# A state-space scan with a Gelu MLP on one core: weight quarters loaded and used in turns, decay rows in four blocks, first B load moved forward

## The chip, the cores and the metric

The kernel runs on one core of one Trainium2 chip. The metric is device time in microseconds (us), taken as the median of several runs. The engines are TensorE (PE in the profile; its weight loads are PEld), VectorE (DVE), ScalarE (ACT), GpSimd (POOL) and SyncE (SP), which here only issues DMAs. Each engine works through its own queue strictly in the order in which the program lists it.

## The reference, cut to what matters

There are 4 batches of 8 heads, 768 positions, 32 values per head and 16 state values. The first half is a scan with decay, the second a two-layer MLP over its output; `B`, `C`, `x` and `a` are inputs.

```python
for c in range(nc):
    cum = np.cumsum(la, axis=-1)
    L = np.exp(cum[:, :, :, None] - cum[:, :, None, :]) * causal
    M = np.einsum('bhin,bhjn->bhij', Cc, Bc) * L
    y = np.einsum('bhij,bhjd->bhid', M, xc) + np.einsum('bhin,bhnd->bhid', Cc, state) * np.exp(cum)[..., None]
    Bx = np.einsum('bhjn,bhjd->bhjnd', Bc, xc) * decay_from_j[:, :, :, None, None]
    state = decay_full[:, :, None, None] * state + np.sum(Bx, axis=2)
h = x @ w_in
g = 0.5 * h * (1.0 + np.tanh(c * (h + 0.044715 * h * h * h)))
return (g @ w_out).astype(np.float32)
```

In the second half `x` is the scan's output as 3072 tokens of 256 values; `w_in` is 256 x 2048 and `w_out` 2048 x 256. All inputs are float32; the kernel multiplies in bfloat16 and sums in float32.

## The kernel before, in words

**Tiles.** Positions are cut into chunks of 128, 6 for each batch, 24 in all. Two chunks (256 tokens) form a unit, so there are 12 units, 3 for each batch. A step is called by its function and its indices: `Y.1` is the second scan product of unit 1, `s1.2.3` the first matmul of the MLP in unit 2, piece 3.

**The scan.** Rows of `a` are clipped and run backwards through a product scan on DVE (`clipq` and `Rq` for chunks 0 to 3 of all batches, from `load_aq`; `clip` and `R` for the long rows, from `load_a`, line 340 for both scans). The results are turned by 32x32 transposes on DVE (`tpq`, `tp2`, `tp6`, line 351), and reciprocals are taken (`recip0`, `recip1`, `recip`). `B` is multiplied by the decay and `C` by its reciprocal (`mulb`, `mulc`, `mul1`, `mul`; for batch 0, chunks 0 to 3 in `BC0[0]`, chunks 4 and 5 in `BC0[1]`). PE transposes the products (`tw`, `T1`, `T`), and copies take them out of PSUM (`ew`, `ce1`, `bh1`, `E`, `F`). For batch 1, `N` turns `B` back and `bn` copies it; batches 2 and 3 are transposed through DRAM by DMA (`load_wr`, `load_tr`, `load_bn`). `G` makes the products of C and B for a unit, four banks of PSUM in two tiles (`ga`, `gb`), `M` multiplies two banks by the triangular mask (line 613, DVE). In unit 0 the second tile goes by ACT (`GE`, a copy) and POOL (`ME`, a select) instead. `D` or `XD` makes the new state terms, `S` adds them up (line 684), `SP` spreads a state over the heads (line 691), and `Y` sums both parts into the PSUM bank `yb`. `yev` copies the result to `xm`, in bfloat16.

**The MLP.** `s1.u.i` is four matmuls (line 717) into one of two buffers `hp` in PSUM, `gelu.u.i` (ACT, line 721) takes them to `gT`. `s2.(u).(k).(q)` is four matmuls of unit u, chunk k, with quarter q of `w_out` (line 735), into a bank `o_ps` (near the end also into `yb`). It needs `gelu.u.2q` and `gelu.u.(2q+1)`. `oev` copies a chunk's sum out of PSUM and `store` writes it. There are 96 steps `s1` and 96 steps `s2`; here they are called pieces. Weights come in quarters of 512 KB (`load_wi`, `load_wo`), each cast to bfloat16 by two steps (`wi.q.k`, `wo.q.k`). `s1.u.0` and `s1.u.1` need quarter 0 of `w_in`, the next two quarter 1, and so on.

**Order.** The steps are issued in an order that is written out by hand in the string `ORDERED`. A letter behind a colon sets the engine (A for ACT, D for DVE, P for POOL, S for SP), otherwise the engine is the one in `add(...)`. `~59` stands for 59 blocks of 128 columns of idle matmuls (`fill`, line 705). `wl`, `bl`, `xl` are load steps on SP's queue, which issues loads, stores and DMA transposes in one row. A DMA's start therefore waits for all that stands ahead of it on SP. From unit 3 to unit 10, `D` and `G` of the next unit are issued inside `Y`.

**What the steps of the change touch.** The order of unit 0 to unit 2 on PE, up to `G.3`, the first product of batch 1, is this:

```
~59 tw.1 tw.2 ~4 tw.0 ~2 G.0 ~1 ppq XX.0 XD.0 ~17 Y.0 XX.1 XD.1 s1.0.0 G.1 s1.0.1 ... s1.0.6 Y.1 pp
s1.0.7 s1.1.0 T1.0 s1.1.1 T1.1 N1 s1.1.2 s1.1.3+10 G.2 s1.1.4 s1.1.5 s2.0.0.0 D.2 s2.0.1.0 s1.1.6
T.1.1 s1.1.7 Y.2 T.1.0 s1.2.0 s1.2.1 N.1 s1.2.2 G.3 D.3
```

`XX` and `XD` for units 0 and 1 leave the transposed `x` and the state terms in PSUM (`XN`), in the bank `o_ps` and in buffers of `hp`. `c_warm` is one Gelu on one column, the first activation of the program; `c_unp` and `c_sel` make constants on DVE.

## Time and profile before

| what | value |
|---|---|
| median of 3 runs | 118.75 us |
| lowest and highest run | 118.48 and 119.01 us |
| span of the profiled execution, first to last instruction | 116.9 us |
| between that span and the median | 1.85 us |
| PE busy | 110.1 us, 1426 matmuls |
| DVE, ACT, POOL busy | 69.4, 72.1, 21.4 us |
| DMA | 15.97 MB, 43007 packets, 36657 of them under 512 B |

The span is the profiled execution's own time as the page gives it; the median also holds what lies around the span. The granted clock of TensorE is 1.000 throughout. The page cuts the span into 40 slices of 2.92 us and gives the busy share of each engine in tenths. The chain is the row of work that ended last, followed back from the last instruction. A time at the left of a line is counted from the span's start.

### The profile page before, as it was taken

How to read it: one execution, taken by the hardware profiler on the slowest of the kernel's cores; microseconds unless marked ns; L12 is line 12 of the kernel's file. 1: busy time of each engine (PE TensorE's matmuls, PEld its weight loads, DVE VectorE, ACT ScalarE, POOL GpSimd, SP SyncE). 2: the span in 40 equal slices, each digit the busy share in tenths (PEclk: the TensorE clock that was granted, in tenths of full speed). 3: DMA queues.
4: the chain of work that ended last, by engine and by line, in shares of the span. 5: the costliest groups of instructions: out<-in, count | busy, mean ns of one | idle time of the engine just before them, and what ended most of it. 6: DMA issues, size and time to landing. Idle time of an engine off the chain costs nothing.

```text
span 116.9 us, 3379 instructions
## 1 busy us (share of the span) xinstructions
PE 110.1 (94%) x1426; PEld 92.0 (79%) x1426; DVE 69.4 (59%) x140; ACT 72.1 (62%) x139; POOL 21.4 (18%) x38
## 2 busy tenths in 40 slices
PE   6988999998899999999999999999999999999990
PEld 2354676776789979989898999889798998999970
DVE  5898899899785936716695583049493462101020
ACT  2249899968486459565766677828465587447501
POOL 7606816908206000052200000000000000000000
PEclk9999999999999999999999999999999999999999
DMA  0999997999983929998407472044201201101113
GB/s 26 228 332 357 281 252 178 208 288 257 305 143 90 185 47 219 213 253 200 72 25 171 121 163 63 0 140 98 40 6 63 71 0 52 43 0 50 45 47 132
DMA packets 43007, 15.97 MB, mean 137 GB/s; under 512 B 36657, under 2 KB 41457, under 8 KB 42993
## 3 DMA queue, kind: packets, MB, share of 16 engines
q1 hardware_dynamic: 42800, 15.64, 56.0%
q8 instruction: 11, 0.18, 0.6%
q10 hardware_dynamic: 192, 0.13, 0.5%
q14 instruction: 4, 0.02, 0.1%
HBM read 11.04 MB, written 3.93 MB: 128 GB/s over the span
## 4 chain that ended last, share of the span: by engine, by line
PE 75%; DMA 8%; DVE 6%; SPq 6%; issue 2%; POOL 1%; ACT 0%; DVEq 0%; POOLq 0%
PE o_ps L735 33%; PE hp L717 30%; DMA bcf<-in_B_dram 8%; PE yb L735 3%; SPq L190 3%; PE ga L603 3%; PE yb L658 2%; DVE m L613 2%; PE yb L667 2%; DVE ce L523 1%; SPq L150 1%; DVE bh L327 1%; DVE bc L484 1%; SPq L159 1%; SPq L183 1%
## 5 line engine op out<-in xcount | busy, mean ns | idle before, releaser
L721 ACT ACTIVATE gT<-hp 128x512 bf16<-128x512 f32 x96 | 54.3, 596 | 25.0 <-PE hp L717 24.6
L717 PE MATMUL hp<-xm,w_in_sb 128*128 128x256 bf16 x384 | 53.3, 273 | 0.6 <-ACT gT L721 0.4
L735 PE MATMUL o_ps<-w_out_sb,gT 128*128 128x256 bf16 x352 | 47.3, 273 | 0.0
L717 PEld LDWEIGHTS <-w_in_sb 128*128 128x128 bf16 x384 | 41.4, 114 | 3.5 <-issue 1.9
L735 PEld LDWEIGHTS <-gT 128*128 128x128 bf16 x384 | 37.0, 98 | 4.9 <-issue 1.1
L327 DVE COPY o_sb<-o_ps 128x256 f32<-128x256 f32 x13 | 5.5, 425 | 23.8 <-PE o_ps L735 20.4
L613 DVE TENSOR_TENSOR m<-ga,tri 128x1024 bf16<-128x1024 f32 x12 | 14.6, 1218 | 0.1
L613 DVE TENSOR_TENSOR m<-gb,tri 128x1024 bf16<-128x1024 f32 x11 | 13.4, 1219 | 0.7 <-PE gb L603 0.7
L323 ACT ACTIVATE o_sb<-o_ps 128x256 f32<-128x256 f32 x9 | 3.5, 385 | 9.2 <-PE o_ps L735 9.2
L705 PE MATMUL yb<-wz 128*128 128x512 bf16 (+3 forms) x23 | 7.6, 481 | 1.1 <-DVE wz L220 1.1
L691 DVE SCALAR_TENSOR_TENSOR sp_new<-s_new,pend,bmask 128x256 bf16<-128x256 f32 x17 | 7.9, 476 | 0.0
L327 DVE CAST xm<-yb 128x512 bf16<-128x512 f32 x6 | 4.1, 687 | 5.8 <-PE hp L636 4.8
L684 DVE SCALAR_TENSOR_TENSOR s_new<-s_new,pend,hp 128x64 f32<-128x64 f32 x13 | 3.6, 279 | 6.4 <-PE hp L636 6.2
L705 PEld LDWEIGHTS <-wz 128*128 128x128 bf16 x26 | 3.0, 120 | 5.1 <-issue 3.2
L667 PE MATMUL yb<-m,x 128*32 128x128 bf16 x192 | 6.1, 220 | 0.0
L603 PE MATMUL ga<-ce,bh 32*128 32x256 bf16 x48 | 4.7, 273 | 1.3 <-DVE bn L327 0.9
L484 POOL TENSOR_TENSOR bc<-bc_t,pt 128x768 bf16<-128x768 f32 x2 | 3.0, 1494 | 13.8 <-DMA bc_t<-in_C_dram 13.7
L658 PE MATMUL yb<-ce,sp_new 128*32 128x128 bf16 x160 | 5.3, 221 | 0.0
L603 PE MATMUL gb<-ce,bh 32*128 32x256 bf16 x48 | 4.7, 273 | 0.0
L735 PE MATMUL yb<-w_out_sb,gT 128*128 128x256 bf16 x32 | 4.6, 273 | 0.0
L667 PEld LDWEIGHTS <-x 128*32 128x32 bf16 x192 | 3.8, 97 | 0.8 <-issue 0.8
L323 ACT ACTIVATE xm<-yb 128x512 bf16<-128x512 f32 x6 | 3.6, 595 | 1.1 <-PE hp L636 1.1
(115 smaller groups left out, 79.5 us busy)
## 6 DMA issues: line engine op xcount, KB each, us to landing
out_dram<-o_sb SPq DMA_DIRECT2D x24, 128.0 KB, 1.9
x_t<-in_x_dram SPq DMA_DIRECT2D x20, 128.0 KB, 3.9
wf<-in_moe_w_in_dram SPq DMA_DIRECT2D x4, 512.0 KB, 6.7
wf<-in_moe_w_out_dram SPq DMA_DIRECT2D x4, 512.0 KB, 5.5
bc_t<-in_C_dram SPq DMA_DIRECT2D x3, 384.0 KB, 5.8
bc_t<-in_B_dram SPq DMA_DIRECT2D x3, 384.0 KB, 5.5
scr<-bc SPq DMA_DIRECT2D x4, 192.0 KB, 2.2
x_t<-in_x_dram SPq DMA_DIRECT2D x1, 512.0 KB, 5.8
```

The source lines that it names most:

```text
L323: nc.scalar.activation(o, i, AF.Copy)
L327: nc.vector.tensor_copy(out=o, in_=i)
L484: (nc.gpsimd if eng == "POOL" else nc.vector).tensor_tensor(out=d["bc16"][:, i], in0=d["bc"].rearrange("p i h (r n) -> p i r h n", r=R6)[: ...
L603: nc.tensor.matmul(out=gbank(g)[:, 256 * k:256 * k + 256], lhsT=bh_of(2 * u + k)[gs], rhs=ce_of(2 * u + k)[gs], start=True, stop=True, til ...
L613: nc.vector.tensor_tensor(out=m_of(u)[:, 2 * i:2 * i + 2].rearrange("p g k e t -> p (g k e) t"), in0=gx[i].rearrange("p g (k t) -> p (g k) ...
L658: nc.tensor.matmul(out=y4[32 * j:32 * j + 32, k, w], lhsT=sp[:, 32 * h:32 * h + 32], rhs=ce_of(gc)[:, h % 2], start=first(j), stop=False, ...
L667: nc.tensor.matmul(out=y4[32 * j:32 * j + 32, k, w], lhsT=X16[u][:, k, 32 * h:32 * h + 32], rhs=m[:, h // 2, h % 2, :], start=first(j), st ...
L691: nc.vector.scalar_tensor_tensor(out=sp_new.rearrange("p (g d) -> p g d", g=4), in0=(XN[0][:, H * D:H * D + 64] if gc == 0 else state[("s" ...
L705: nc.tensor.matmul(out=t[:, 0:m * 128], lhsT=wz, rhs=w3.to_broadcast([128, m, 128]), start=True, stop=True, skip_group_check=True)
L717: nc.tensor.matmul(out=hp[:, j * T:(j + 1) * T], lhsT=w_in_k[:, w, q, k], rhs=xm[:, w, u * T:(u + 1) * T], start=(w == 0), stop=(w == 1))
L721: nc.scalar.activation(gts[u][:, 2 * i:2 * i + 2], hps.pop((u, i)).rearrange("p (j t) -> p j t", j=2), AF.Gelu_apprx_tanh)
L735: nc.tensor.matmul(out=ops[gc], lhsT=gts[u][:, fi, k * Q:(k + 1) * Q], rhs=w_out_sb[:, fi, :], start=(fi == 0 and (u > 0 or k == 0)), stop ...
```

## The change

**Loads.** On SP's queue the load of B for the first four chunks (`load_bc0.0`) is issued first, ahead of two of the four loads of the first decay rows (`load_aq.1`, `load_aq.3`; the other two are on ACT's queue). The quarters of `w_in` and `w_out` then take turns with other loads: `wi.0 wi.1 wo.0 bc1(C) wi.2 bc1(B) wi.3 wo.1 x.2(half) wo.2 x.2(half) bc.1(C) bc.1(B) x.3(half) wo.3`. Before, it was `wi.0 wi.1 wi.2 wi.3 bc1(C) bc1(B) wo.0 x.2 bc.1(C) bc.1(B) x.3 wo.1 wo.2 x.4 wo.3`. A unit's `x` becomes two steps.

**Long decay rows.** `a_t` held 64 rows of 384; now it holds four blocks of 32 rows in 128 partitions, 192 positions each, with the last two chunks behind them in columns 256 to 383. Four DMAs load it, all on ACT's queue. `tp2` is one transpose where it was four, `tp6` one of 128x192 where it was four of 32x192, and the reciprocals of batches 1 to 3 are three steps.

**Uses.** In units 0 and 1 `s2` goes by quarters: both chunks of a unit share a bank (unit 0 `o_ps`, unit 1 `yb`) and take quarter 0, then quarter 1, and so on. `XX.1` goes to the banks of `gb`. `M` of unit 0 on `gb` is one bank on DVE (`MD.0.3`) and one by ACT and POOL; for unit 1 both banks of `gb` go by ACT and POOL. `Y.0` is issued in halves. `mulb` is cut in two, `x4` in four.

**Engines.** Among others, `c_unp` and the second half of `c_sel` go to ACT, the mask `bmask` to DVE; `wi.0.0`, `wi.2.1`, `wi.3.1`, `wo.1.0`, `castx.2`, `ce1`, `bh1`, `bn1`, `mul.1.1` and `E.1.1` are on DVE. `c_warm` stands between `Y.10` and `gelu.9.1`, so the first activation is a Copy. The order of all later units is new as well.

The order on PE up to `G.3` is now this (`Yw` is half of `Y.0`):

```
~47 tw.0 tw.1 tw.2 ~6 G.0 ppq ~12 XX.0 XD.0 G.1 Yw.0.0 Yw.0.1 s1.0.0 s1.0.1 XX.1 XD.1 s1.0.2 s1.0.3
s2.0.0.0 s2.0.1.0 s1.0.4 s1.0.5 T1.1 Y.1 T1.0 pp s1.0.6 s1.0.7 G.2 s2.0.0.1 s1.1.0 s1.1.1 s2.0.1.1
s1.1.2 N1 s2.0.0.2 s2.0.1.2 D.2 s1.1.3 s1.1.4 Y.2 s1.1.5 s1.1.6 T.1.1 s2.1.0.0 s1.1.7 s1.2.0 s2.1.1.0
s2.1.0.1 T.1.0 s1.2.1 s2.1.1.1 s2.1.0.2 s2.1.1.2 N.1 s1.2.2 s2.0.0.3 D.3 G.3
```

The diff, cut to its core:

```diff
+c_wz load_aq.2 load_aq.0 c_ident c_tri c_sel c_sub c_m4 load_bc0.0 load_a.0 c_zero load_aq.1
+load_aq.3 c_az c_ends load_bc0.1 load_x4 c_unz clipq Rq tpq recip0 load_a.2 c_cz mulb.0 load_a.1
+c_unp ~47 mulb.1:P mulc.0 mulc.1:P load_a.3 c_selp tw.0 tw.1 load_wi.0 tw.2 x4.0:P ew.0.0:A ew.0.2
+peq load_wi.1 x4.1:P ew.1.0 ew.0.1 ew.1.1:A ~6 G.0 c_bmask:D load_wo.0 load_bc1.1 ew.1.2 load_wi.2
+load_bc1.0 ppq x4.2 x4.3 pendq MD.0.3 c_m16 GE.0.2 ~12 XX.0 xn.1 M.0.0 xn.0 XD.0 SP.0 S.0.0
+load_wi.3 G.1 ME.0.2 Yw.0.0 GE.1.3 wi.0.0:D Yw.0.1 yev.0.1.2 wi.0.1 load_wo.1 load_x.2.0 GE.1.2
...
+s1.0.2 gelu.0.1 ME.1.2 load_wo.2 load_x.2.1 xn.3 S.1.0 tp2 s1.0.3 c_par s2.0.0.0.o wi.2.1:D S.1.1
+wi.2.0 recip1 s2.0.1.0.o pe SP.1 SP.2 mul1.1:P gelu.0.2 xn.2 gelu.0.3 s1.0.4 load_bc.1.1 s1.0.5
+mul1.0:P T1.1 ce1.1:D wi.3.0 wi.3.1:D Y.1 gelu.0.4 wo.1.1 T1.0 pp ce1.0:D load_bc.1.0 gelu.0.5 pend
+bh1:D load_x.3.0 s1.0.6 yev.1.0.2 wo.2.0 wo.1.0:D s1.0.7 load_wo.3 G.2 tp6 gelu.0.6 gelu.0.7
...
-    a_t = const.tile([64, HS], FP32, name="a_t")
+    a_t = const.tile([128, AL], FP32, name="a_t")
...
     def f_tp2():
-        for k in range(4):
-            turn(rt0[1][32 * k:32 * k + 32], r_t[32:64, Q + 64 * k:Q + 64 * k + 64], 2)
+        turn(rt0[1], r_t[:, 2 * Q:2 * Q + Q // 2], 2)
...
+    def f_tp6():
+        turn(rt, r_t[:, 0:QL], R6)
...
+            XN[c] = gx[1][:, k] if u else pso.tile([128, 512], FP32, name="o_ps") if k == 0 else psh.tile([128, 512], FP32, name="hp")
...
+    def f_MD(u, g):
+        nc.vector.tensor_tensor(out=m_of(u)[:, g].rearrange("p k e t -> p (k e) t"),
+                                in0=gbank(g).rearrange("p (k t) -> p k t", t=Q), in1=tri_b(4), op=ALU.mult)
...
+            if u < 2:
                 if k == 0:
-                    ops["0"] = pso.tile([128, 512], FP32, name="o_ps")
+                    ops["u"] = yb if u else pso.tile([128, 512], FP32, name="o_ps")
...
-        for k, q in [(k, q) for q in range(4) for k in range(2)] if u == 0 else [(k, q) for k in range(2) for q in range(4)]:
+        for k, q in [(k, q) for q in range(4) for k in range(2)] if u < 2 else [(k, q) for k in range(2) for q in range(4)]:
```

## The prediction

> **What bounds the kernel now.** I read the page's busy slices first, then a table of busy time by stage, then the chain, then the DMA landings.

> ```profile
> PE   6988999998899999999999999999999999999990
> DVE  5898899899785936716695583049493462101020
> DMA  0999997999983929998407472044201201101113
> ```

> Each digit is 2.92 us in tenths. PE is full from the eleventh slice on; the first ten hold its only gaps, and there DVE and DMA are full.

> ```profile
> 10.00:12.46 2.46, 2.46 (x101) 1.33 (x93) 1.97 (x5) 2.37 (x6) 1.97 (x3) 1.00 1.04 394
> 12.46:18.90 6.44, 5.99 (x78) 4.52 (x78) 5.88 (x14) 5.86 (x13) 2.52 (x5) 1.00 0.96 213
> 18.90:24.00 5.10, 4.84 (x49) 3.50 (x49) 4.50 (x8) 4.67 (x11) 4.29 (x6) 1.00 1.15 212
> 24.00:29.69 5.69, 4.51 (x73) 3.67 (x72) 5.60 (x9) 4.09 (x7) 2.79 (x5) 1.00 1.03 293
> 29.69:113.90 84.21, 84.18 (x1080) 75.25 (x1079) 43.43 (x76) 50.61 (x94) 5.01 (x5) 1.00 0.44 100
> ```

> Columns: length, then PE, PEld, DVE, ACT, POOL busy. From 29.69 PE is busy 84.18 of 84.21 us, so **the end is the start of G.3 plus what PE still has to do then**. Just before, DVE is busy 5.60 of 5.69. The chain shows what G.3 waits for:

> ```profile
> 27.74 1.44 DVE ce L523 x2
> 29.17 0.48 DVE bn L327
> 29.69 0.28 PE ga L603 x2
> ...
> 37.91 1.75 PE o_ps L735 x16
> ```

> DVE's `F.1` and `bn.1` release G.3. The last line prices a piece: 16 matmuls in 1.75 us, four in 0.4375.

> **Pieces ahead of G.3.** By the two orders on PE, 19 steps `s1` and 2 `s2` stood ahead of G.3; now 19 and 13, and `D.3` (0.17, chain row at 30.09). PE's last matmul ends at 113.88, 84.19 after G.3. Of that, 11 x 0.4375 + 0.17 = 4.98 moves ahead. If G.3 started when it does now, the gain would be 4.98. All depends on how much later it starts. I follow the new queues with durations of these rows.

> **The first loads.** Landings, read as issue plus time to landing: `bc0` 5.2 and 6.4, `x4` 8.6, the quarters of `w_in` 9.9, 11.5, 12.9, 14.3, `bc1` 14.7 and 16.65, `wo.0` 18.2, `bc.1` 21.75 (C) and 23.3 (B), `wo.1` 26.2, `wo.2` 27.6. The stream is gapless, so a load costs the step between landings: 1.2 for a half of bc0, 2.2 for x4, 1.4 for a quarter, 1.15 for a half of bc1, 0.75 for half of an x, 1.7 for a half of bc.1. B goes out at 0.81, 0.92 before the first bc0 load now (1.73, landing 3.5 later), so it lands at 4.3 and the stream runs about 0.8 earlier. The two aq loads behind it lie between 3.5 (issue 1.73 plus their 1.8 unhindered) and 4.5 (behind all of B); I take 4.4. DVE now reaches `clipq` at 4.25 straight from `unp`, which goes to ACT; so clipq starts 0.15 later, while `mulb` and `mulc`, halved between DVE (0.42) and POOL (0.62), win 0.35. ACT takes `unp` (four at about 0.2) and `selp` while it waits for `tw` until 6.99 anyway. G.0 comes at 7.9 (now 8.13). x4 lands at 7.9 instead of 8.6, and halves of `x4`, `M.0` and `Y.0` run side by side: s1.0.0 at about 11.85 (now 12.46). The four `load_a` cost ACT's queue two more issues (0.32 to 0.44 each) before 6.9, where it idles; the `x` halves cost SP nothing new, each unit had two DMAs.

> **The weights in turns.** By the same steps: wi.0 9.3, wi.1 10.7, wo.0 12.2, wi.2 14.8 (1.9 later than now), wi.3 17.3 (3.0 later), wo.1 18.9 (7.3 earlier), wo.2 21.1, bc.1 23.5 (C, 1.75 later) and 25.1 (B), wo.3 27.3. So unit 0 waits for wi.3 and its casts: s1.0.6 at 18.1. Until then PE runs six s1 pieces and two s2. Then stand 24 pieces and 2.2 of G.2, Y.2, D, T and N before G.3: 12.7 us, which makes 30.8 the earliest G.3.

> **DVE up to G.3.** Removed:

> ```profile
> 16.93 1.94 DVE L351 STREAM_TRANSPOSE rt<-r_t 32x192 f32<-32x192 f32 x6
> 19.29 1.07 DVE L351 STREAM_TRANSPOSE rt<-r_t 32x192 f32<-32x192 f32 x2
> ```

> These eight become a 128x64 (0.24, as 32x64) and a 128x192 (0.54, as 32x192): -2.2; a cost by partitions is excluded by 128x128 at 0.41. Reciprocals 1.03 become two of 0.44 before F.1: -0.15. `M.1` on gb leaves: -1.2. `xn.0`, `yev.2`: -1.1. Added: MD 0.63, bmask about 0.7 (a reduce like 0.37 and a copy), `yev` half 0.42, casts wi.0.0, wi.3.1, wo.1.0, castx.2 1.7 (wi.2.1 replaces wi.3.0), ce1 0.82, bh1 and bn1 0.8, mul.1.1 0.95 (was POOL), E.1.1 0.96 (was ACT): +7.0. Net +2.3, less the 0.6 idle that DVE has at 22: 1.7 by the sum. Followed in order: SP.2 ends 17.2, M.2 22.2, SP.4 24.1, mul.1.1 starts 24.55 (after C landed at 23.5), E.1.1 27.0, mul.1.0 27.95, E.1.0 29.5, F.1 30.95, bn.1 31.45; G.3 at 31.65, with PE ready at 31.45. Both arrive together: **1.96 later than now**. ACT and POOL have idle stretches on this way and set nothing.

> **Two prices that the trace doesn't hold.** First, DVE casts beside POOL casts:

> ```profile
> 1.92 1.19 DVE L282 COPY selp<-sel 128x128 f32<-128x128 f32 x1
> 15.75 0.42 DVE L327 CAST w_in_sb<-wf 128x512 bf16<-128x512 f32 x1
> 27.65 1.52 DVE L523 TENSOR_SCALAR ce<-ch,par 128x768 bf16<-128x768 bf16 x2
> ```

> The cast at 15.75 ran with POOL idle. The selp copy ran beside a POOL memset, and this F pair beside POOL casts, where one of its form takes 0.41 at best: a stretch of 0.35 each. Of five DVE casts, wi.2.1, wi.3.1 and wo.1.0 are released by the same load as a POOL cast: 3 x 0.35 = 1.05; but F.1 now comes when POOL has finished its casts: -0.70. I take +0.4; bounds -0.7 and 5 x 0.77 = 3.85 (selp's 1.19 against 0.42). [...]

> Second, the first activation is now a Copy. Before, one table load (1.28, at 2.21) stood ahead of the Gelu of `c_warm`. If the load for Copy doesn't serve Gelu, a second one of 1.28 stands before gelu.0.0. The row of pieces up to s1.0.6 has 0.85 of slack, which leaves 0.4. Bounds 0 and 1.28; I take 0.4. [...]

> **After G.3.** The units' order is new, but PE's work is the same and ACT and DVE are half idle (43.43 and 50.61 of 84.21). The tightest place I find is Y.5: 12 pieces (5.25) after Y.4, against 4.9 of DVE work (S, two M, two SP, F.2). I add nothing. The fills dropped (about 2 us) stood in gaps. The tail is the same.

> **Sum.** G.3 at 31.65 + 0.4 + 0.4 = 32.45, 2.76 later; 2.76 - 4.98 = -2.2. The span of 116.9 becomes 114.7; with the 1.85 that lie between span and median, 118.75 becomes **116.5**.

> **Rivals.**
> - *PE's bound.* If casts don't collide, one table load suffices and loads are 0.5 earlier, G.3 comes at 30.3 to 31, 1.0 later than now: 114.7. For it: 30.8 above; against: DVE needs 31.65 by itself.
> - *Late loads.* bc.1 has 1 MB more ahead of it. If C lands 2.8 later than I think (26.3; SP's issues stall up to 3.4 us in this stretch), mul.1.1 waits 1.75 more, G.3 comes at 34.2 and gives back most of the gain: 118.3. Against it: the stream's own steps.
> - [...] At DVE, 11 to 31 us, all five casts pay 0.77: G.3 at 31.65 + 0.4 + 3.85 = 35.9, 6.2 later, 1.2 slower: 120.0. It decides from 0.52 for each cast (4.98 - 1.96 - 0.4 = 2.6). For it: the selp row; against: the F pair.
> - *No effect.* If the moved s2 pieces only wait for wo.1 and wo.2, G.3 slides by their whole length: 118.75. Against it: both land before their pieces are due. I count it with late loads.

> **Chances.** Forecast (115.4 to 117.6) 0.5, PE's bound 0.16, late loads or no effect 0.14, the port 0.2. A difference under 0.5% (0.6 us) can't be told from none here. Half of the late loads fall within it: faster 0.73, same 0.07, slower 0.20. The range reaches from 114.3 to 119.4: the low end with all bounds favourable, the high one half-way into the port's case.

> **What would show it.** s1.0.0 near 11.85; wi.3 cast at 17.3 to 18.1; two L351 rows on r_t; DVE casts of 0.4 to 0.8; one or two table loads; 32 pieces before G.3 and G.3 near 32.4; no PE gap after it. The prediction fails if G.3 starts after 34.1 (29.69 + 4.98 - 0.6), or if PE has gaps behind it.

## The result, and the profile after

The changed kernel is **slower**: 124.67 us median (123.83 to 125.02, 5 runs) against 118.48 (118.03 to 119.01, 5 runs) of the kernel before on the same chip. The ratio is 1.0509, 95% interval 1.0467 to 1.0551. The forecast was 116.5 us, the range 114.3 to 119.4. The profiled execution took 123.83 us with a span of 122.1. Ratios here and below are of undisturbed runs alone, so they can differ from the quotient of two medians, and in the table of the experiments a dash stands where the profiled execution was disturbed.

The busy slices of the changed kernel, 3.05 us each, with the clock that TensorE was granted:

```profile
PE   6938769989999999999999999999999999999990
DVE  4366366999977959457635765846693662102020
PEclk9995555699999999999999999999999999999999
DMA  3699999799708953999997583000004400200032
```

From the tenth slice on PE is as full as before. The loss is in the first nine: PE falls to 3 tenths in the third slice, DVE in the second and third to 3 and 6 where it had 8 and 9, and the clock stands at half for four slices. Before, the clock row held 9 throughout.

The same table by stage (length, then PE, PEld, DVE, ACT, POOL busy with counts, granted clock, DMA share, GB/s), the last bound moved to the new start of G.3:

```profile
6.00:9.00 3.00, 0.91 (x9) 0.45 (x8) 1.86 (x5) 0.44 (x4) 1.33 (x2) 1.00 0.97 247
9.00:12.46 3.46, 2.84 (x21) 1.21 (x19) 2.53 (x7) 2.67 (x9) 1.37 (x6) 0.58 0.97 293
12.46:18.90 6.44, 4.75 (x81) 2.47 (x80) 3.42 (x8) 3.62 (x8) 3.57 (x6) 0.50 1.04 321
18.90:24.00 5.10, 5.10 (x62) 3.32 (x61) 4.00 (x12) 3.48 (x7) 3.21 (x6) 0.57 0.93 247
24.00:39.74 15.74, 15.43 (x213) 12.91 (x212) 13.73 (x25) 9.90 (x20) 4.14 (x6) 1.00 0.75 168
39.74:119.10 79.36, 79.25 (x1036) 70.91 (x1028) 42.11 (x75) 50.78 (x96) 6.44 (x6) 1.00 0.45 93
```

G.3 starts at 39.74 instead of 29.69. Behind it PE is without gaps, as before (79.25 of 79.36), and the rest of the span is 82.4 instead of 87.2. So **4.8 us did move ahead of G.3, and G.3 came 10.05 later**, where 2.76 were forecast. Between 6 and 9 us PE works 0.91 of 3.00, where the kernel before had 2.50:

```profile
6.00:9.00 3.00, 2.50 (x29) 1.48 (x27) 2.97 (x10) 1.66 (x5) 0.31 (x1) 1.00 1.11 336
```

What holds PE up in the changed kernel stands in its timeline (start, duration, engine, line, operation; in brackets the idle time before and who ended it):

```profile
3.48 0.39 SPq L152 DMA_DIRECT2D bcf<-in_C_dram  x1
5.04 0.23 DVE L370 TENSOR_SCALAR acq<-aq_t 128x128 f32<-128x128 f32 x1 [2.34 <-DMA aq_t<-in_a_dram]
8.26 0.42 DVE L450 TENSOR_TENSOR cz<-bcf,pt 128x256 bf16<-128x256 f32 x1 [1.10 <-DMA bcf<-in_C_dram]
8.82 0.32 ACTq L180 DMA_DIRECT2D a_t<-in_a_dram  x1
9.19 0.31 ACT L356 ACTIVATE selp<-sel 128x128 f32<-128x128 f32 x1 [2.75 <-POOL cz L450]
10.70 0.40 PE L636 MATMUL ga<-ce,bh 32*128 32x256 bf16 x2 [0.53 <-DVE ce L360]
17.64 1.86 PE L758 MATMUL hp<-xm,w_in_sb 128*128 128x256 bf16 x8 [0.94 <-DVE xm L360]
```

SP's queue, whose waits the page lists apart, shows what the first line stood for:

```profile
SPq L152 <- DMA aq_t<-in_a_dram: 1.1, 1, 1.1
```

The load of C, behind B and two loads of `aq` on SP, could go out at 2.3 and waits 1.1 us for the landing of a load of `aq`, whose data it doesn't need. The trace's records of the DMA issues show why. The changed kernel has 81 issues on the two queues, and each names one of eight completion semaphores (100, 102 and 104 to 109), which come in turn over both queues together. The four loads of `aq`, B and three loads of `a` have the eight first, and their records name no wait (the third load of `a` goes out after C, at 4.02, but has its semaphore already). C is the ninth: its record names 100, like that of the first load of `aq`, and a wait for 100. That load of `aq` landed at 3.46, and C went out at 3.48. It lands 4.7 later, at 8.16, and `mulc` at 8.26 is late. The fourth load of `a` shares 108 with the third, which landed at 8.74: a wait for 108 ends on **ACT's** queue at 8.78, the load goes out at 8.82, and ACT's constants and its copies for G.0 stand behind it: the bracket on `selp` names POOL, but the DMA issue just ahead of it on ACT is what ended at 9.14. G.0 comes at 10.70, s1.0.0 at 17.64 and runs at half clock: eight matmuls in 1.86 us, where a piece of four had 0.4375.

### The profile page after: what moved, and what is told of

The parts are those of the page before. It is cut to its first block, busy times and chain, and to the rows that moved or that the text cites. A ratio compares the mean times of both kernels' runs of the same rounds, so it can differ in the third digit from the quotient of the medians.

```text
span 122.1 us, 3377 instructions
## 1 busy us (share of the span) xinstructions
PE 113.2 (93%) x1417; PEld 92.9 (76%) x1417; DVE 69.9 (57%) x137; ACT 72.7 (60%) x142; POOL 23.3 (19%) x47
## 4 chain that ended last, share of the span: by engine, by line
PE 84%; DMA 7%; DVE 2%; ACT 2%; POOL 1%; issue 1%; SPq 0%; POOLq 0%
PE hp L758 36%; PE o_ps L776 28%; PE yb L776 5%; DMA bcf<-in_C_dram 4%; PE ga L636 4%; PE yb L696 3%; PE yb L705 3%; DMA aq_t<-in_a_dram 2%; DMA out_dram<-o_sb 1%; PE yb L746 1%; PE gb L604 1%; PE o_ps L604 1%; POOL cz L450 1%; DVE w_in_sb L360 1%; PE hp L673 1%
## 5 line engine op out<-in xcount | busy, mean ns | idle before, releaser
L758 PE MATMUL hp<-xm,w_in_sb 128*128 128x256 bf16 x384 | 55.2, 279 | 1.3 <-DVE xm L360 0.9
L758 PEld LDWEIGHTS <-w_in_sb 128*128 128x128 bf16 x384 | 41.9, 115 | 4.4 <-issue 1.1
L776 PE MATMUL o_ps<-w_out_sb,gT 128*128 128x256 bf16 x320 | 44.5, 274 | 0.0
L360 DVE COPY o_sb<-o_ps 128x256 f32<-128x256 f32 x11 | 4.7, 424 | 20.9 <-PE o_ps L776 18.8
L646 DVE TENSOR_TENSOR m<-gb,tri 128x1024 bf16<-128x1024 f32 x10 | 12.2, 1217 | 0.0
L776 PE MATMUL yb<-w_out_sb,gT 128*128 128x256 bf16 x64 | 8.9, 273 | 0.0
L746 PE MATMUL yb<-wz 128*128 128x512 bf16 (+2 forms) x17 | 7.3, 603 | 1.1 <-DVE wz L239 1.1
L746 PEld LDWEIGHTS <-wz 128*128 128x128 bf16 x17 | 2.3, 145 | 4.1 <-issue 3.0
L356 ACT ACTIVATE xm<-yb 128x512 bf16<-128x512 f32 (+1 forms) x8 | 4.6, 570 | 0.8 <-PE hp L673 0.4
L358 POOL CAST w_out_sb<-wf 128x512 bf16<-128x512 f32 x6 | 4.1, 715 | 4.6 <-DMA wf<-in_moe_w_out_dram 4.6
```

Source lines behind the costliest of these rows:

```text
L356: nc.scalar.activation(o, i, AF.Copy)
L358: nc.gpsimd.tensor_copy(out=o, in_=i)
L360: nc.vector.tensor_copy(out=o, in_=i)
L646: nc.vector.tensor_tensor(out=m_of(u)[:, 2 * i:2 * i + 2].rearrange("p g k e t -> p (g k e) t"), in0=gx[i].rearrange("p g (k t) -> p (g k) ...
L746: nc.tensor.matmul(out=t[:, 0:m * 128], lhsT=wz, rhs=w3.to_broadcast([128, m, 128]), start=True, stop=True, skip_group_check=True)
L758: nc.tensor.matmul(out=hp[:, j * T:(j + 1) * T], lhsT=w_in_k[:, w, q, k], rhs=xm[:, w, u * T:(u + 1) * T], start=(w == 0), stop=(w == 1))
```

## The experiments

Each was timed against the kernel before on its own chip. The medians, ratios with 95% intervals, and the starts of three steps in the profiled execution:

| kernel | median us | ratio to before | G.0 | s1.0.0 | G.3 |
|---|---|---|---|---|---|
| before | 118.48 | | 8.13 | 12.46 | 29.69 |
| after | 124.67 | 1.0509 (1.0467 to 1.0551) | 10.70 | 17.64 | 39.74 |
| a_late | 122.58 | 1.0355 (1.0284 to 1.0425) | 9.29 | 15.29 | 36.90 |
| aq_first | 126.17 | 1.0657 (1.0579 to 1.0735) | 12.05 | 18.98 | 41.62 |
| fill | 123.85 | 1.0484 (1.0403 to 1.0566) | 10.85 | 16.31 | 38.90 |
| table | 124.41 | 1.0478 (1.0385 to 1.0572) | - | - | - |
| late_fill | 120.34 | 1.0161 (1.0087 to 1.0235) | 9.58 | 14.82 | 35.90 |
| late_xd | 121.90 | 1.0188 (1.0110 to 1.0267) | - | - | - |
| all_undone | 118.98 | 1.0073 (1.0029 to 1.0117) | 9.30 | 14.05 | 34.66 |
| before_cold | 121.10 | 1.0260 (1.0212 to 1.0308) | 8.81 | 14.11 | 31.89 |
| loads_as_before | 118.70 | 1.0005 (0.9966 to 1.0044) | 9.08 | 13.83 | 34.23 |
| behind | 123.18 | 1.0360 (1.0280 to 1.0441) | 8.88 | 13.63 | 33.19 |
| before_bfirst | 125.07 | 1.0415 (1.0283 to 1.0547) | 10.83 | 16.98 | 35.37 |
| bfirst_a_early | 119.23 | 1.0073 (1.0049 to 1.0097) | 9.71 | 13.52 | 30.12 |
| a_early | 121.14 | 1.0208 (1.0160 to 1.0256) | 11.02 | 15.77 | 36.05 |

The first four kernels change one thing each in the changed kernel: the place of the `a` loads, the order of the first loads, the idle matmuls, the table load.

**a_late**

```diff
-... recip0 load_a.2 c_cz mulb.0 load_a.1 / c_unp ~47 mulb.1:P mulc.0 mulc.1:P load_a.3 c_selp tw.0 tw.1 load_wi.0 tw.2
+... recip0 c_cz mulb.0 / c_unp ~47 mulb.1:P mulc.0 mulc.1:P c_selp tw.0 tw.1 load_wi.0 load_a.2:S load_a.1:S load_a.3:S tw.2
```

> The changed kernel, with load_a.2, load_a.1 and load_a.3 issued by SP behind wi.0 instead of by ACT ahead of the first copies. In the changed trace SP issues the first C load (bc0.C) at 3.48, 1.15 after the DMA before it, released by the landing of the first aq load: eight DMAs were already on their way. Here bc0.C is one of the first eight. Theory 1 (late first loads: the wait costs the start, and the late start lets PE run idle and lose its clock): bc0.C is issued near 2.4 and lands near 6.5 instead of 8.16, G.0 comes near 9 instead of 10.70, the mean granted clock rises from 0.944, and the time falls from 124.7 to 119 to 121. Theory 2 (the clock alone, from fewer idle matmuls): the clock still falls to 0.5 near 9.6, time 123 to 124. Theory 3 (second table load and a new order of bank users): G.0 earlier but s1.0.0 to G.3 as long as before, 123.

The loss falls by 1.7 us (from 124.67 - 118.48 to 122.58 - 118.07), and neither C nor ACT is held any longer. Which of the two waits weighs more was not separated. The time misses the expected range; the clock fell all the same, from about 8 to 11 and from about 15 to 21 us.

**aq_first**

```diff
-... c_m4 load_bc0.0 load_a.0 c_zero load_aq.1 load_aq.3 c_az
+... c_m4 load_aq.1 load_aq.3 load_bc0.0 load_a.0 c_zero c_az
```

> The changed kernel with load_aq.1 and load_aq.3 ahead of the first B load, as before the change. bc0.C still has eight DMAs ahead of it. clipq starts near 3.6 instead of 5.04, and bc0.C is released earlier, near 2.8. Theory 1: the front gains about 1, G.0 near 9.7, time 123 to 124 unless the clock holds; if the clock holds, 119 to 121. Theory 2 (clock from fewer idle matmuls): no more than the earlier start, 123.5. If B ahead of the decay rows is itself the cause of the loss: 120 or less.

Slower still. C goes out at 2.61, but ACT was now held by the fourth load of `a` until 10.17 and G.0 came at 12.05. Putting B back mends nothing as long as ACT is held.

**fill**

```diff
-c_unp ~47 ... tw.0 tw.1 ... ew.1.1:A ~6 G.0
+c_unp ~62 ... tw.0 ~16 tw.1 ... ew.1.1:A ~16 G.0
```

> The changed kernel with more idle matmuls on PE: 62 blocks instead of 47 at the start, 16 new ones between tw.0 and tw.1, 16 instead of 6 ahead of G.0. Loads and all else as changed. Theory 2 (the clock is the loss): the granted clock stays at 1.0 through 23 us, pieces cost 0.44 instead of 0.87 there, and the time falls by 4 to 5, to about 120. Theory 1 (late loads make most of the loss by themselves): G.0 still near 10.7, s1.0.0 near 15.5, time 122 to 123.

No gain that can be told from none (the interval overlaps that of the changed kernel). The clock held to about 13 us instead of 9.6 and fell then: the gaps that idle matmuls have to fill go on up to s1.0.0 (at 16.31; PE is busy 1.51 of 3.00 us from 9 to 12, and 2.25 and 2.05 in the next two stretches of that length).

**table**

```diff
-... c_az c_ends load_bc0.1 ... Y.10 c_warm gelu.9.1
+... c_az c_warm c_ends load_bc0.1 ... Y.10 gelu.9.1
```

> The changed kernel with c_warm (the Gelu on one column) issued right behind c_az, so that it is the first activation again. One table load instead of two: the one of 1.28 at 18.15 goes. It also holds ACT's later load_a issues back, so bc0.C has fewer than eight DMAs ahead. Theory 1: like the run with the late a loads, bc0.C near 2.4, G.0 near 9, time 118.5 to 121. Theory 3 (second table load): 1.3 less, 123.4, with the clock still at 0.5. Theory 2: 123 to 124, clock falls.

One table load instead of two, and within the intervals nothing gained: it is not what the kernel waits for.

The next four combine. late_fill and late_xd add one edit to a_late each; all_undone adds all of them, with a warm-up first and `mulc.1` on DVE; before_cold takes idle matmuls out of the kernel before.

**late_fill**

```diff
-c_unp ~47 ... tw.0 tw.1 ... ~6 G.0 ... ~12 XX.0 ... load_wi.3 G.1 ... s1.0.0 clip
+c_unp ~66 ... tw.0 ~9 tw.1 ... ~12 G.0 ... ~4 XX.0 ... load_wi.3 ~12 G.1 ... s1.0.0+14 clip
```

> The run with the late a loads, and idle matmuls so spread that PE has something to do from 1 to 15 us: 66 blocks at the start, 9 between tw.0 and tw.1, 12 ahead of G.0, 4 instead of 12 ahead of XX.0, 12 ahead of G.1, 14 inside s1.0.0. In the run with the late a loads (122.6) the clock fell to 0.5 at 8.3 and again from 15 to 21.3; there the 12 blocks ahead of XX.0 took 1.2 while the x4 casts were ready. Clock theory: the granted clock stays at 1.0, XX.0 starts near 10.3 instead of 11.44, the pieces from 15 to 21 cost 0.44, time 118 to 119.5. Rival (the order of the first steps makes the loss, the clock hides behind it): 121.5 to 122.5 with the clock at 1.0.

A further 2.4 us of the loss are gone (122.58 - 118.07 to 120.34 - 118.20). This and the next two rows are the clock rows of late_fill, of fill, and of a_late:

```profile
PEclk9999999999999999999999999999999999999999
```

```profile
PEclk9999555799999999999999999999999999999999
```

```profile
PEclk9976955999999999999999999999999999999999
```

Of the three only late_fill keeps the clock. Its gain over a_late is that of the clock together with the eight blocks fewer ahead of `XX.0`, which the edit moves as well; before_cold, below, shows the clock by itself.

**late_xd**

```diff
-... XX.0 xn.1 M.0.0 xn.0 XD.0 SP.0
+... XX.0 XD.0 xn.1 M.0.0 xn.0 SP.0
```

> The run with the late a loads, with XD.0 issued ahead of the copies xn.1 and xn.0, as before the change. In the changed trace XD.0 starts 0.75 late, released by ACT's copies out of the same banks. If that order costs: XD.0 follows XX.0 directly, 0.9 earlier, s1.0.0 near 14.4 instead of 15.29, time 121.7 against 122.6. If not: 122.6, s1.0.0 at 15.3. The clock theory expects the clock to fall here too, so no more than 1.

Its four runs scatter from 119.84 to 122.84: 0.7 below a_late by the medians, 1.7% by the ratios. That XD.0's place gains something is likely by the ratios, how much is open.

**all_undone** (against late_fill)

```diff
-... c_az c_ends load_bc0.1 ... mulc.0 mulc.1:P c_selp ... ~4 XX.0 xn.1 M.0.0 xn.0 XD.0 SP.0 ... Y.10 c_warm gelu.9.1
+... c_az c_warm c_ends load_bc0.1 ... mulc.0 mulc.1 c_selp ... ~4 XX.0 XD.0 xn.1 M.0.0 xn.0 SP.0 ... Y.10 gelu.9.1
```

> The changed kernel with the late a loads, the spread idle matmuls, XD.0 ahead of its copies, c_warm first (one table load) and mulc.1 on DVE instead of POOL. Weights in turns, use by quarters, four blocks of decay rows and B ahead of half the first decay rows stay. If the loss lies in the start and the clock and not in the weights and quarters: s1.0.0 near 12.5, G.3 near 33, time 116 to 117.5, below the kernel before. If the weights in turns hold unit 0 up, as the rival of late loads says: 118.5 to 120, with PE waiting for the casts of wi.2 and wi.3.

Of the loss of 6.2 us (124.67 - 118.48) 0.8 is left (118.98 - 118.20). The stretch from s1.0.0 to G.3 is 20.61, where the prediction has 32.45 - 11.85 = 20.60. That they agree to 0.01 is luck: the prediction counts 0.4 for a second table load, which this kernel doesn't have, and doesn't have the 14 idle blocks that stand in `s1.0.0` here.

**before_cold**

```diff
-mulc.0 ~59 tw.1 ... mulb ~4 tw.0 ... c_par ~2 G.0 ... SP.0 ~17 Y.0
+mulc.0 ~35 tw.1 ... mulb tw.0 ... c_par G.0 ... SP.0 Y.0
```

> The kernel before with fewer idle matmuls: 35 blocks instead of 59 at the start, none ahead of tw.0, G.0 and Y.0 (4, 2 and 17 before). Nothing else is changed. Clock theory: PE idles for more than half of the time from 4 to 12 us, the clock falls to 0.5 within that stretch, XX, XD and the first s1 pieces take twice as long, and the time rises from 118.1 to 120.5 to 122. If the idle matmuls only fill gaps: 118.0 to 118.3.

These matmuls compute nothing, and without 47 of their blocks the kernel before takes 2.9 us more. The table row from 12 to 18 us, and the first piece in the timeline:

```profile
12.00:18.00 6.00, 5.96 (x88) 3.24 (x82) 4.78 (x8) 4.10 (x9) 2.40 (x4) 1.00 0.95 230
```

```profile
14.11 1.04 PE L717 MATMUL hp<-xm,w_in_sb 128*128 128x256 bf16 x4
```

Four matmuls take 1.04 us; in the kernel before the first piece took 0.60. Yet the view gives the granted clock as 1.00. The clock's record in this trace has its first entry at 17.1 us, and just there the pitch of the matmuls goes from 0.21 to 0.11 us. Ahead of the first entry (5.8 us in the kernel before) the pitch tells the clock, not the row.

**loads_as_before** (all_undone, and the first loads as in the kernel before)

```diff
-c_wz load_aq.2 load_aq.0 ... load_bc0.0 load_a.0 c_zero load_aq.1 load_aq.3 c_az c_warm c_ends load_bc0.1 load_x4
+load_aq.0 load_aq.1 load_aq.2 load_aq.3 c_wz load_bc0.1 load_bc0.0 ... c_zero c_az c_warm c_ends load_x4
-load_wi.0 load_a.2:S
+load_wi.0 load_a.0:S load_a.2:S
```

> As the last kernel (a rows late, idle matmuls spread, XD.0 ahead of the copies, one table load, mulc.1 on DVE), with the front loads back as they were before the change: the four quarter loads aq ahead of everything, C first on ACT and B on SP behind aq, load_a.0 late with the other a loads. Theory (the order of the first loads costs what is left at the start): clipq 4.25 instead of 4.58, the first C lands by about 5.7 instead of 7.1, G.0 at 8.1 to 8.6 instead of 9.30; x4 lands no earlier (8.6), so XX.0 at 9.4 to 9.9 and s1.0.0 at 13.0 to 13.5 instead of 14.05; the stretch s1.0.0 to G.3 stays 20.6, so G.3 at 33.6 to 34.1 and the time 117.9 to 118.5, at or just below the kernel before. Rival (x4 and the DVE casts set G.0 to s1.0.0 whatever the first loads do): G.0 moves, s1.0.0 stays within 0.2 of 14.05 and the time within 0.3 of 118.98.

118.70 us: **no difference from the kernel before** (1.0005). In the kernel as run, C too is on SP's queue, ahead of B, as it was before the change, and not on ACT's as the expectation says. Theory and rival both miss by a little: `clipq` starts at 3.57, but `mulb` waits 0.45 for B, which lands at about 6.1, and G.0 comes only 0.2 earlier; s1.0.0 stands at 13.83 and G.3 at 34.23, with 82.8 behind it. Against the kernel before, G.3 comes 4.5 later and the rest is 4.4 shorter (87.2 - 82.8).

**behind** (loads_as_before, with the eleven s2 pieces moved to right behind G.3)

```diff
-tp6 gelu.0.6 gelu.0.7 s2.0.0.1.o s1.1.0 ... s2.0.1.1.o ... s2.0.0.3.o D.3 oev.0:D G.3 s1.2.3
+tp6 gelu.0.6 gelu.0.7 s1.1.0 ... D.3 G.3 s2.0.0.1.o s2.0.1.1.o ... s2.0.0.3.o oev.0:D s1.2.3
```

> As loads_as_before, with the eleven s2 pieces of units 0 and 1 (ten of them and s2.0.0.3) and oev.0 moved from ahead of G.3 to right behind it. Theory of the prediction (what is ahead of G.3 fills time in which PE would wait for DVE anyway, and PE has no gap behind G.3): G.3 comes some 3.4 earlier than in loads_as_before (17.2 from s1.0.0 as in the kernel before, instead of 20.6), the time from G.3 to the end grows by the pieces, 4.8, to 88.3, and the whole is slower than loads_as_before by about 1.4. Rival A (the pieces cost PE their full time where they stand): G.3 comes 4.8 earlier and the time is within 0.4 of loads_as_before. Rival B (DVE sets G.3 alone, the pieces are free there): G.3 stays and the time is 4.8 longer.

Tables of the stretch from s1.0.0 to G.3, first of loads_as_before, then of behind:

```profile
13.83:34.23 20.40, 19.57 (x281) 16.05 (x281) 17.99 (x38) 13.19 (x27) 9.47 (x13) 1.00 1.02 232
```

```profile
13.63:33.19 19.56, 15.78 (x235) 11.88 (x235) 18.09 (x37) 12.80 (x27) 9.80 (x13) 0.98 1.08 254
```

PE's work shrinks by 3.8, DVE's doesn't, and the stretch by 0.84 only: **without the pieces DVE sets G.3**, and the pieces fill time in which PE would wait. With them the two arrive nearly together, as the prediction said: in loads_as_before `bn.1` is done at 33.84, and PE comes to G.3 0.38 later.

```profile
33.28 0.56 DVE L360 COPY bn<-ga 128x768 bf16<-128x768 bf16 x1 [0.47 <-PE ga L562]
34.22 0.28 PE L636 MATMUL ga<-ce,bh 32*128 32x256 bf16 x2
```

That is nearer to rival B than to the 3.4 of the theory. The loss of 4.5 us in the whole is not all that price: `oev.0`, moved with the pieces, stands ahead of `M.3` on DVE and keeps it idle for 6.80 us behind G.3.

```profile
39.69 0.42 DVE L360 COPY o_sb<-o_ps 128x256 f32<-128x256 f32 x1 [6.80 <-PE o_ps L776]
```

**before_bfirst** (the kernel before with one load moved)

```diff
-load_aq.0 load_aq.1 load_aq.2 load_aq.3 c_wz ... c_zero load_bc0.0
+load_bc0.0 load_aq.0 load_aq.1 load_aq.2 load_aq.3 c_wz ... c_zero
```

> The kernel before with one edit: on SP's queue B's first load stands ahead of both of its aq loads (1 and 3); the C load stays third on ACT's queue. Theory (B first alone costs little, as C stays where it was): clipq 4.6 instead of 4.25, G.0 8.1 to 8.5, the time 0 to 0.4 above the kernel before. Rival (B ahead of half the decay rows is what puts the start late): G.0 over 0.8 later and the time 0.8 or more above.

By the ratio 4.9 us (3.4 to 6.5), most of what the whole change costs: the rival's size, and far over mine. The four runs scatter from 123.02 to 127.61, so the size is rough. The edit also moves C, which stands on SP's queue behind B and not on ACT's: it goes out at 2.40 instead of 1.73. The rows of its timeline and its clock:

```profile
4.71 0.32 ACTq L162 DMA_DIRECT2D a_t<-in_a_dram  x1
...
10.09 0.35 DVE L337 TENSOR_SCALAR ac<-a_t 64x384 f32<-64x384 f32 x1 [1.59 <-DMA a_t<-in_a_dram]
10.37 0.41 DVE L327 COPY ce<-hp 128x256 bf16<-128x256 bf16 x1
...
10.83 0.28 PE L603 MATMUL ga<-ce,bh 32*128 32x256 bf16 x2 [2.25 <-DVE ce L327]
```

```profile
PEclk9998555999999999999999999999999999999999
```

The second load of `a`, issued at 3.15 in the kernel before, waits until 4.71. By the turn of the eight semaphores it now shares one with the first load of `a`, which was issued at 1.75 and landed 2.9 later, at about 4.65. The second load then lands 5.4 later, with x and the weights in transfer beside it (3.8 at most in the kernel before). DVE reads it ahead of a copy that G.0 needs, so PE waits 2.25 us, and its clock falls to 0.50.

**bfirst_a_early** (before_bfirst, and that load moved ahead, off the shared semaphore)

```diff
-load_x4 Rq tpq recip0 c_cz mulc.0 ~59 tw.1 load_wi.0 c_warm load_a.1:A
+load_x4 load_a.1:A Rq tpq recip0 c_cz mulc.0 ~59 tw.1 load_wi.0 c_warm
```

> As before_bfirst (the kernel before with B's first load ahead of both aq loads of SP's queue), with load_a.1 right behind load_x4 instead of behind the first weight loads and the table load, so that it no longer shares its completion semaphore with load_a.0. Theory (the shared semaphore did it: the load was held to 4.71 and landed at 10.09, with the copies for G.0 behind its reader on DVE): the load is issued by about 2.3 and lands by 7 to 8, DVE does not wait for it, G.0 at 8.9 to 9.2 instead of 10.83, and the time is 119.2 to 121, at most half of the 6.3 us left. Rival (B's place as such: acq 0.8 late, PE idle meanwhile and its clock down): G.0 moves but the time stays above 122.

119.23 us, and this is the row of its timeline that answers to 10.09 above:

```profile
8.98 0.34 DVE L337 TENSOR_SCALAR ac<-a_t 64x384 f32<-64x384 f32 x1
```

The load goes out at 2.22 and lands at about 5.7. DVE waits no more for it, the clock stays full, and of 4.9 us 0.9 are left by the ratio, though `clipq` starts at 5.60, even later than the 5.05 of before_bfirst. So B's place as such costs 0.9, and the late load of `a`, with the clock that falls after it, about 4. The edit moves the load ahead of the table load as well, so it goes out sooner than in the kernel before (3.15), too.

**a_early** (loads_as_before, with the `a` loads back on ACT)

```diff
-load_bc0.1 load_bc0.0 c_ident ... c_az c_warm c_ends load_x4 c_unz ... load_wi.0 load_a.0:S load_a.2:S load_a.1:S load_a.3:S tw.2
+load_bc0.1 load_bc0.0 load_a.0:A c_ident ... c_az c_warm load_x4 load_a.2:A load_a.1:A load_a.3:A c_ends c_unz ... load_wi.0 tw.2
```

> As loads_as_before, with the four a loads back on ACT's queue: a.0 behind aq, the other three behind the table load, so that SP's queue is free for the first weight loads 2.3 us earlier. Theory (after the start is mended, the weight loads behind the a loads are on the path, as the chain of loads_as_before has two of them, 6.56 and 7.04 long, up to 17.04): the third w_in load lands 1 to 2 earlier, G.3 0.5 to 1 earlier than 34.23, time 117.5 to 118.3, below the kernel before. Rival (DVE sets G.3 whatever the weights do): G.3 stays within 0.3 and the time within 0.4 of 118.7. Rival (ACT held by the shared semaphores, as in the changed kernel): ACT's first copies start late, G.0 behind 9.08, time above 119.2.

The second rival. ACT's queue issues no load between 3.90 and 7.79, held by an earlier load's landing, and the constants behind it wait:

```profile
7.79 0.32 ACTq L176 DMA_DIRECT2D a_t<-in_a_dram  x1
8.63 0.63 ACT L356 ACTIVATE unp<-sub 128x32 bf16<-128x32 bf16 x4 [4.04 <-DMA a_t<-in_a_dram]
```

B, too, lands at about 8.2 instead of 6.1, with two loads of `a` beside it. G.0 comes at 11.02, and 2.4 us are lost (121.14 against 118.70) with the clock at full. No version here beats the kernel before.

## Why the prediction was wrong

**The book-keeping of the end held.** The prediction's last span, 114.7 - 32.45 = 82.25 behind G.3, measured 82.36. PE has no gap there.

**The stretch from s1.0.0 to G.3 held where the clock was full.** 20.60 by the prediction's times; 21.08 in late_fill, with both table loads, and 20.61 and 20.40 in all_undone and loads_as_before, with one. All three have 14 idle blocks more in it, so it held to about half a us, not to 0.01. That DVE would set G.3 without the pieces is shown by behind, where G.3 came only 1.04 earlier. The two transposes took 0.24 and 0.51 (0.24 and 0.54 forecast).

**The step that failed is "The first loads".** G.3 came 7.29 later than 32.45, in three parts:

- *G.0 at 7.9*: it came at 10.70, 2.80 later. "The four load_a cost ACT's queue two more issues before 6.9, where it idles" counted issues and not their waits: the first three issues took 1.32, 0.72 and 0.46, the fourth was held until 8.82, and by the three ahead of it C went out at 3.48 and landed at 8.16, where the prediction's steps (B at 4.3, 1.2 for a half) put it near 5.5. The aq loads landed so that `clipq` started at 5.04, beyond the upper bound of 4.5. Moving three of the loads and nothing else (a_late) brought G.0 to 9.29; the other 1.4 stayed, as no kernel with the change has G.0 ahead of 8.88.
- *G.0 to s1.0.0, 3.95*: it took 6.94, 2.99 more. The prediction has no term for the clock. "The fills dropped (about 2 us) stood in gaps" is right, but with fewer fills and a late G.0 PE stood idle, the clock fell to 0.50, and `XX`, `Y` and 12 blocks of fill ran at half speed. With the clock at full the way took 4.75 (all_undone, loads_as_before), so some 0.8 of the 2.99 was mis-sized in the steps themselves. "Halves of x4, M.0 and Y.0 run side by side" didn't hold for the two copies of `Y.0`: ACT's starts at 16.75, DVE's at 17.16, and DVE waits for ACT's. Both read the bank `yb` and write `xm`; which of the two makes it wait is not shown.
- *s1.0.0 to G.3*: 22.10, 1.50 more, at half clock up to about 23 us.

By the experiments, the place of the `a` loads is worth 1.7 us, and the clock with the blocks moved for it 2.4 (fewer idle matmuls alone cost the kernel before 2.9). XD.0, the table load and `mulc.1` make another 1.4 together by the medians of late_fill and all_undone, whose intervals overlap, and were not separated. The first loads in their old order take back what is left (1.0073 to 1.0005, intervals overlapping as well).

**The rest.** The second table load was there, and not seen in the time (124.41 without it, in the run table):

```profile
18.15 1.28 ACT L762 ACT_TABLE_LOAD   x1
19.45 1.08 ACT L762 ACTIVATE gT<-hp 128x512 bf16<-128x512 f32 x2
```

Two loads, at 4.51 and at 18.15, as the prediction took it; gelu.0.0 starts at 19.45, right behind the 1.28.

Of the five casts on DVE one stretched beside a cast on POOL (0.84 for 0.42, at 25.36) and four took 0.41 or 0.42. Two `SP` at 23.27 stretched too, which the prediction didn't count: 1.63 us, where two alone take 0.96. The pair in `F.1` took 0.74 instead of 1.52, as forecast.

Of the rivals, none was this one. "Late loads" had the right kind, a transfer behind others, but at bc.1 and not at the first C, and 118.3 for it. The chance of 0.20 for slower ("the port" among the chances) rested alone on the rival in which all five DVE casts pay 0.77; one of the five paid, 0.42. The point that the prediction named for its own failure, G.3 after 34.1, is what happened.

**Would the change have paid with a good start?** In loads_as_before it doesn't: 4.4 us move ahead of G.3 and G.3 comes 4.5 later, 1.4 of it ahead of s1.0.0 and 3.2 behind it (20.40 instead of 17.23). Of the 3.2, 2.3 remain without the moved pieces (19.56 in behind), where DVE is busy for 18.09. That s1.0.0 could be had at 11.85 has not been shown by any kernel.

## What to carry to other kernels

Count the DMAs of all queues together ahead of the first work, and ask for each of them which landing it must wait for before it is issued. In the kernel before the ninth in the turn was the first quarter of `w_in`, which went out at 3.61, and the load that had its semaphore had landed at 2.76; in the changed kernel, with more loads of `a` on ACT's queue, it was C, which was held for 1.1 us. An issue that was held on ACT's queue until 8.82 held ACT's computing too: `selp` came at 9.19. Before idle matmuls are dropped or the work ahead of a gap is made later, look at how long PE would stand idle in the first 20 us: a G.0 that came 1.6 later cost 0.9 with the clock kept (bfirst_a_early), one that came 2.7 later cost 4.9 with the clock down (before_bfirst). At the start, read the clock from the pitch of the matmuls and not from the row.

## What the runs showed of the hardware that was not expected

```profile
11.24:14.65 3.41, 3.41 (x47) 1.67 (x48) 2.72 (x5) 2.57 (x6) 1.83 (x3) 0.50 1.00 307
14.65:18.07 3.42, 3.42 (x74) 1.81 (x76) 1.22 (x4) 1.51 (x4) 1.79 (x3) 0.50 0.66 164
18.07:21.48 3.41, 3.41 (x23) 2.01 (x20) 2.86 (x4) 1.98 (x4) 0.00 (x0) 0.50 1.01 213
```

  So a step without gaps was followed by the full clock in the changed kernel, and by half of it in before_bfirst: PE's busy share alone doesn't tell when the clock comes back. Fewer idle matmuls, with the clock at half up to 17.1 us, cost the kernel before 2.6% (before_cold).
- **The clock's record is missing at the start**: the row gives 1.00 ahead of the first entry at 17.1 us, where a piece takes 1.04 instead of 0.60 (before_cold).
- **Loads landed later in more company.** The 48 KB of the second load of `a` took 3.8 us at most in the kernel before and 5.4 in before_bfirst; B's first 256 KB landed about 3.9 after their issue in loads_as_before and 6.0 in a_early, where only loads of `a` stood beside them in addition.
